# Reordered small work in a software-pipelined attention and Fourier kernel: maskings, a last fold, square roots, input requests and the work behind the last product

## The chip, the cores and the metric

The kernel runs on one core of one Trainium2 chip. The metric is the device time of an execution in microseconds (us). Of several executions the median counts; beside it there is one execution that was profiled, and all durations of single instructions come from that one.

## The reference

Threshold attention, whose output goes through a Fourier mixing, a layer norm and a two-layer channel network. The sizes are B = 8 batches, H = 8 heads, S = 576 tokens, D = 64, so the width is 512, and the hidden width of the network is 2048. All data are float32.

```python
scores = q @ k.transpose(0, 1, 3, 2) / sqrt(64)             # [8, 8, 576, 576]
scores = where(scores >= max(scores, -1) - tau, scores, -1e9)
attn = exp(scores - max(scores, -1))
attn = attn / (sum(attn, -1) + 1e-9)
x = (attn @ v).transpose(0, 2, 1, 3).reshape(8, 576, 512)

u = x + real(fft(fft(x, axis=1), axis=2))
un = (u - mean(u, -1)) / sqrt(var(u, -1) + 1e-6)
out = u + maximum(un @ w1, 0) @ w2                          # w1 512x2048, w2 2048x512
```

## The kernel before, in words

**One loop over attention steps, with the rest fitted in between.** Two heads form a pair; there are 32 pairs (four a batch). The 576 queries of a pair are cut into five steps: t = 0 to 3 take 128 queries of each head, t = 4 the last 64 of both. So a batch has 20 steps, numbered i = 0 to 159 over all, with n = i // 5 the pair and t = i % 5. Batch 0 (`step`) and batch 1 (`second_batch`) also load and prepare the weights. From batch 2 on (about 400 us into the profile, when `late` is set) the loop at L1587 runs, once per step, with these parts in this order:

1. `scores` (L427): q times k into PSUM buffers `sc`, of which there are two.
2. `softmax_first`: VectorE takes the row maxima (L506), ScalarE the exponentials (L512), from the same `sc`.
3. `values_in_parts`: after t = 2 and t = 4 the weights of a half pair times v (`pv`, L627), copied by ScalarE to `x` or, for the batch's first pair, `x_first` (L634).
4. `fill()`, explained below.
5. `softmax_second`: VectorE masks the exponentials (L527; it reads `sc` as well and so sets it free) and makes the reciprocals of the sums.
6. `weights_in_parts`: TensorE transposes the weights of the step before (`pe` and `pw`, L578 and L596), ScalarE copies them out (L584, L598). A second `fill()` lies between its parts.
7. `softmax_third`: ScalarE divides (L540). At t = 1 `prep_ends` copies the last queries, at t = 2 `scale_q` scales the next pair's q, at t = 3 `prep_pair` transposes the next pair's k and q on VectorE (L398 to L401) and then calls `load_pair(n + 1)`.
8. A third `fill()`.

`load_pair` (L134) issues eight transfers for q and k of a pair, `load_v` (L149, L152) four for v. All of them stand in the queue of the SyncE engine, in program order, along with the weight loads and the stores of the output. `q_in` and `k_in` have one buffer each, which the transposes read; `v_in` has two.

**Folding and mixing.** After each pair `fold_rows` makes the symmetric sums and differences of x that the Fourier products need, into `f`. It is a generator, moved on by `fold_more()` at fixed places. It runs on GpSimd (POOL in the profile), but for the last pair of each batch on VectorE; that last one is spread over the first steps of the next batch, and at step i % 20 == 2 `start_batch` makes the batch's mixing available. `mixing(b)` first combines the four chunks of `f` on VectorE (`fold_chunks` L709 and L710, then L735, L731, L740), then multiplies by the table over the width (`py`, L750), over the tokens (`pa`, L767), forms `low` and `high` in a shared buffer `tmp` (L787, L788), and adds x, on GpSimd, into `u_t`, the transposed u (the inner function `add`, L790 and L794), chunk by chunk: chunks 0 and 3 in the first of two rounds, 1 and 2 in the second.

**Channel network in the background.** The tokens are cut into nine groups of 512, g = 0 to 8. Group 0 is computed plainly (`channels`), the others by `two_level`, which replaces each product by seven on sums of quarters, twice over. A *first stretch* makes 28 blocks of the hidden layer (`ph`, L1161). Its right operands, differences of quarters of `u_t`, are made by `u_form` on GpSimd (L1085; one goes to `t_room`), and VectorE empties the banks by additions (L1098). A *second stretch* has seven products of seven blocks each (`po`, L1278), emptied by ScalarE copies or VectorE additions (L1292, L1295) into five vectors `v_u`, `v_11`, `v_22`, `v_21`, `v_12` of 7 x 128 columns. `gather` (L1209) sums the seven columns of a vector to results, `finish` adds these to u (L861), `rows.store` sends the rows out (L868). The left operands are made ahead by `l2_forms` (L1142, VectorE and GpSimd) and `l1_form` (L1119). Small jobs are hung at slots of a product (`at_slots(at, (jn, ...), jobs)`, run after block jn of product number at), or put into the list `pending`, of which `tick()` does two after each block of the next first stretch. `rows.load` (L834 to L843) transposes u back and takes its mean and variance; `rows.factors` takes the square root (L850), calls one exponential so that the table of ScalarE is back (L853), and the reciprocal on VectorE (L854).

The weight forms of `two_level` lie in DRAM (`f1`, `f2`) and come in loads of four blocks, 1 MB each (`w<-f`, L1034), into three buffers in turn. `block` asks for a load two ahead.

**What sets the order.** The instruction order is written out by hand: each engine works through its own instructions in program order, and waits for others by semaphores. `fill()` adds a share to a budget and does one part of the mixing, then blocks of the background (`work`) until the budget is spent:

```python
    def fill():
        nonlocal budget, spent
        budget += per_slot
        if mixes:
            mix(1)
        while work and spent < budget and work[0][0] < mixed:
            done = next(work[0][1], None)
```

A group of batch b can start when that batch's mixing is done (`mixed`). Behind the last step, the last mixing and the rest of the groups are done by the loop at L1635, with no attention work left between.

PSUM has four banks for everything but the scores (`mm`), taken in turn.

Of the kernel before, what the change touches and what calls it, by code (L numbers as in the profile page):

```python
# [47 lines left out]
def kernel(  # L48
# [12 lines left out]
    nc = tc.nc  # L61
# [4 lines left out]
    NPAIR = H // 2  # L66
# [324 lines left out]
    def prep_pair(n):  # L391

        q_raw, k_raw = loaded.pop(n)
        kT = sb.tile([128, D + S], FP32, tag="kT", name="kT")
        nc.vector.transpose(kT[:, D : D + S], k_raw[:, :])  # L398
        nc.vector.transpose(kT[64:128, 0:D], k_raw[64:128, 512:S])
        qT = sb.tile([128, S], FP32, tag="qT", bufs=1, name="qT")  # L400
        nc.vector.transpose(qT[:, :], q_raw[:, :])  # L401
        heads[n] = (qT, kT, v_in[n % 2])
        if n + 1 < B * NPAIR:
            load_pair(n + 1)
# [314 lines left out]
    def mixing(b):  # L719
# [58 lines left out]
        for t in range(2):  # L778
# [9 lines left out]
            nc.vector.tensor_tensor(out=high, in0=pa[:, 0:KH], in1=sin, op=ALU.add)  # L788
            def add(c, rows, first, second, eng=nc.gpsimd):
                eng.tensor_tensor(  # L790
# [269 lines left out]
    def two_level(g, rows):  # L1060
# [22 lines left out]
        def u_form(out_, in0, in1):  # L1083
            for c in range(2):
                nc.gpsimd.tensor_tensor(  # L1085
                    out=out_[:, c], in0=in0[:, c], in1=in1[:, c], op=ALU.subtract
                )
# [111 lines left out]
        for _ in forms:  # L1199
            pass  # L1200
        while pending:
            tick()
        if g == 1:
            for part in range(4):
                s1_part(part)
# [20 lines left out]

        def finish(i, n, v):
            v = v.rearrange("p (j n) -> p j n", n=128)
            cols = slice(256 * n, 256 * n + 256)
# [35 lines left out]
        at_slots(2, (0, 1, 2, 3, 4), gather(P, v_11))  # L1265
        at_slots(4, (0, 2), finish(0, 0, v_11))
        at_slots(
            5, (0,), [lambda: P.tensor_tensor(out=v_12, in0=v_u, in1=v_22, op=ALU.add)]
        )
        at_slots(6, (0, 1), [plus(P, v_22, v_u), plus(P, v_21, v_u)])  # L1270
        for at, m in enumerate(L1):
            for jn, j in enumerate(J):
                if jn in (0, 4):
                    bank = ps.tile([128, 512], FP32, tag="mm", bufs=4, name="po")
                to = bank[:, 128 * (jn % 4) : 128 * (jn % 4 + 1)]
                right_ = block(g, True, 7 * at + jn)
                for s in range(4):
                    nc.tensor.matmul(  # L1278
                        to, lefts[m][j][:, s], right_[:, 128 * s : 128 * (s + 1)],
                        start=jn in (0, 4) and s == 0, stop=s == 3, skip_group_check=True,  # L1280
                    )
                if jn in (3, 6):
                    size = 512 if jn == 3 else NV - 512
                    src = bank[:, 0:size]

                    def here(v):
                        return v[:, 0:512] if jn == 3 else v[:, 512:NV]

# [4 lines left out]
                    else:  # L1293
                        to = here(v_12 if m == 3 else v_u)
                        V.tensor_tensor(out=to, in0=to, in1=src, op=ALU.add)  # L1295
                for job in side.get((at, jn), ()):
                    job()
                if jn == 3 and at < 4:
                    rows.load((2, 3, 0, 1)[at])
                    if at == 3:  # L1300
                        rows.factors()
                    yield ND * 128
# [3 lines left out]
            if m != 3:  # L1306
                yield 2048
        last = g == NG - 1
        for v in (v_22, v_21, v_12):
            pending.extend(gather(V if last else P, v))  # L1310
        pending.extend(finish(1, 1, v_22))
# [3 lines left out]
        pending.append(stores(0, 1))  # L1315
        if g == NG - 1:
            while pending:
                tick()
        yield 2048

    pending = []

    def tick():

        for _ in range(2):
            if pending:
                pending.pop(0)()

# [14 lines left out]

    late = []


# [5 lines left out]

    def fill():
        nonlocal budget, spent
        budget += per_slot
        if mixes:
            mix(1)
        while work and spent < budget and work[0][0] < mixed:
            done = next(work[0][1], None)
            if done is None:  # L1360
                work.pop(0)
            else:
                spent += done

    total = B * per_batch
# [221 lines left out]
    for i in range(2 * per_batch, total + 3):  # L1587
# [16 lines left out]
        if i % per_batch == 2:  # L1604
            while folds:
                fold_more()
            start_batch(i // per_batch - 1)
        if t == 1 and n + 1 < B * NPAIR:
            load_v(n + 1)
        fill()  # L1610
        if t == 1:
            folds.append(fold_rows(n - 1))
        if i < total:
            softmax_second(i)
        weights = weights_in_parts(i - 1) if i <= total else iter(())
        next(weights, None)
        if t > 2 or i % per_batch == 1:
            fold_more()
        fill()
        if i % per_batch == 1:  # L1620
            fold_more()
        next(weights, None)
        if i < total:
# [5 lines left out]
            if t == 3 and n + 1 < B * NPAIR:  # L1629
                prep_pair(n + 1)  # L1630
        if i % per_batch == 1:
            fold_more()
        fill()
    per_slot = cost(0) / 40
    while mixes or work:  # L1635
# [47 lines left out]
```

## Time and profile before

| | |
|---|---|
| median of 9 runs | 1615.22 us (1612.22 to 1617.65) |
| profiled execution | 1617.93 us, of which its span is 1616.2 us |
| TensorE clock granted, mean over the span | 0.984 |
| instructions | 27099 |
| busy: TensorE matmul, TensorE weight load | 1543.8 us (96%), 1191.5 us (74%) |
| busy: VectorE, ScalarE, GpSimd | 1085.0 (67%), 907.1 (56%), 827.3 us (51%) |
| transfers | 239.05 MB, on average 148 GB/s |

In the profile PE stands for TensorE, PEld for its weight loads, DVE for VectorE, ACT for ScalarE, POOL for GpSimd, SP for SyncE; SPq is the issue of a transfer in SyncE's queue. A line as `PE sc L427 <- DVE e L527: 6.4, 6, 2.7` in the list of waits says: TensorE, about to do the product at line 427 into `sc`, waited for VectorE's operation at line 527 that writes `e`, 6.4 us in all, 6 times, the longest 2.7 us. In the timeline a line has start, duration, engine, source line, operation and the number of instructions put together in it; in brackets stands the idle time ahead of it and what ended that.

### The profile page before, as it was taken

The numbers are of one execution on the slowest core, as the hardware profiler recorded it, in microseconds if no ns is written. First come the engines' busy times: TensorE is split into PE (matmuls) and PEld (weight loads), VectorE is DVE, ScalarE is ACT, GpSimd is POOL, SyncE is SP. The second block draws the span as 40 slices with busy tenths as digits, with TensorE's granted clock in tenths as the row PEclk, the third lists the DMA queues.
The fourth block names the chain that finished last, engine by engine and source line by source line (L and its number), as shares of the span: only waits on it lengthen the run. The fifth ranks groups of instructions, "written<-read, shape, count | busy, mean of one in ns | idle before, by whom it ended". The sixth has DMA issues, their size and how long they took to land.

```text
span 1616.2 us, 27099 instructions
## 1 busy us (share of the span) xinstructions
PE 1543.8 (96%) x9770; PEld 1191.5 (74%) x9770; DVE 1085.0 (67%) x2141; ACT 907.1 (56%) x1873; POOL 827.3 (51%) x1035
## 2 busy tenths in 40 slices
PE   8999889999999999999999999999999999899997
PEld 4555445555787777877787878787887778879997
DVE  7997786855867666776567566856676656536446
ACT  5775665544664566656766576666665665123121
POOL 6784664034454542646254724554264526547746
PEclk9999999999999999999999999999999999999999
DMA  6423221555945344644455345545453435446655
GB/s 159 128 57 114 74 75 36 178 153 155 280 133 209 107 143 137 190 122 133 140 156 156 118 128 153 175 122 161 127 180 108 145 112 179 167 152 234 235 196 187
DMA packets 245499, 239.05 MB, mean 148 GB/s; under 512 B 196947, under 2 KB 214869, under 8 KB 225014
## 3 DMA queue, kind: packets, MB, share of 16 engines
q1 hardware_dynamic: 242854, 237.02, 47.7%
q8 instruction: 78, 1.28, 0.3%
q10 hardware_dynamic: 2512, 0.30, 0.2%
q14 instruction: 55, 0.45, 0.1%
HBM read 207.50 MB, written 29.62 MB: 147 GB/s over the span
## 4 chain that ended last, share of the span: by engine, by line
PE 74%; DVE 14%; ACT 4%; DMA 3%; issue 2%; POOL 2%; SPq 1%; DVEq 0%; ACTq 0%; POOLq 0%
PE ph L1161 23%; PE po L1278 18%; PE pv L627 8%; PE sc L427 7%; PE pw L596 6%; PE po L899 3%; PE ph L875 2%; DVE e L467 2%; PE sc L433 1%; PE py L750 1%; DVE neg L506 1%; ACT e L512 1%; PE pa L767 1%; DVE e L527 1%; DVE neg L451 1%
## 5 line engine op out<-in xcount | busy, mean ns | idle before, releaser
L512 ACT ACTIVATE e<-sc,neg 128x576 f32<-128x576 f32 x216 | 158.6, 734 | 137.4 <-DVE neg L506 137.4
L1278 PE MATMUL po<-w,w_all 128*128 128x128 f32 x1792 | 230.0, 278 | 4.0 <-DMA w<-f 4.0
L506 DVE TENSOR_REDUCE neg<-sc 128x1 f32<-128x576 f32 x216 | 154.0, 750 | 111.9 <-PE sc L427 106.1
L1278 PEld LDWEIGHTS po<-w,w_all 128*128 128x128 f32 x1792 | 214.9, 194 | 12.9 <-issue 11.0
L1098 DVE TENSOR_TENSOR hs<-ph,hs 128x512 f32<-128x512 f32 (+1 forms) x128 | 105.2, 822 | 172.8 <-PE ph L1161 118.0
L1107 POOL TENSOR_TENSOR w<-hs 128x512 f32<-128x512 f32 x32 | 41.7, 1307 | 323.0 <-ACT hs L1103 249.7
L427 PE MATMUL sc<-kT,qT 64*128 64x288 f32 x1024 | 175.7, 436 | 16.1 <-DVE e L467 8.5
L596 PE MATMUL pw<-ident,e 128*128 128x128 f32 x1152 | 170.8, 275 | 14.0 <-ACT x_first L634 5.7
L1161 PE MATMUL ph<-u_t,w 128*128 128x256 f32 x768 | 180.5, 381 | 0.7 <-DMA w<-f 0.5
L598 ACT COPY e_t<-pw 128x512 f32<-128x512 f32 x256 | 147.7, 592 | 51.9 <-PE pw L596 50.5
L527 DVE SCALAR_TENSOR_TENSOR e<-sc,thr,e 128x576 f32<-128x576 f32 x216 | 168.1, 811 | 12.4 <-ACT thr L516 12.4
L540 ACT ACTIVATE e<-e,den 128x576 f32<-128x576 f32 x216 | 157.7, 776 | 30.3 <-DVE den L534 29.6
L596 PEld LDWEIGHTS pw<-ident,e 128*128 128x128 f32 x1152 | 135.6, 141 | 33.2 <-ACT x_first L634 7.5
L1161 PEld LDWEIGHTS ph<-u_t,w 128*128 128x128 f32 x768 | 141.2, 190 | 23.5 <-issue 4.9
L1161 PE MATMUL ph<-w_all,w 128*128 128x256 f32 x672 | 156.4, 382 | 0.0
L427 PEld LDWEIGHTS sc<-kT,qT 64*128 64x128 f32 x1024 | 95.8, 188 | 74.4 <-issue 31.9
L1161 PEld LDWEIGHTS ph<-w_all,w 128*128 128x128 f32 x672 | 123.8, 190 | 21.7 <-issue 6.4
L1103 ACT ACTIVATE hs<-hs 128x512 f32<-128x512 f32 (+1 forms) x96 | 74.1, 771 | 113.9 <-DVE hs L1098 112.9
L1209 POOL TENSOR_TENSOR w_all<-w_all 128x128 f32<-128x128 f32 (+2 forms) x161 | 117.5, 747 | 23.7 <-DVE w_all L1295 10.2
L1278 PE MATMUL po<-w,hs 128*128 128x128 f32 x960 | 126.9, 279 | 0.0
L1278 PEld LDWEIGHTS po<-w,hs 128*128 128x128 f32 x960 | 116.9, 194 | 5.1 <-issue 3.3
L790 POOL TENSOR_TENSOR u_t<-x,tmp 128x289 f32<-128x289 f32 (+1 forms) x47 | 34.5, 734 | 98.9 <-DVE tmp L787 98.9
(217 smaller groups left out, 2984.4 us busy)
## 6 DMA issues: line engine op xcount, KB each, us to landing
w<-f SPq DMA_DIRECT2D x152, 1024.0 KB, 4.9
hs<-in_moe_w_ch_dram SPq DMA_DIRECT2D x23, 512.0 KB, 4.6
q_in<-in_q_dram SPq DMA_DIRECT2D x128, 72.0 KB, 2.4
out_dram<-u SPq DMA_DIRECT2D x36, 256.0 KB, 2.3
k_in<-in_k_dram SPq DMA_DIRECT2D x124, 72.0 KB, 2.5
v_in<-in_v_dram SPq DMA_DIRECT2D x64, 128.0 KB, 2.5
f<-w SPq DMA_DIRECT2D x14, 512.0 KB, 3.3
f<-w SPq DMA_DIRECT2D x7, 1024.0 KB, 4.3
```

What stands on the lines that cost most here:

```text
L427: nc.tensor.matmul(sc[j][:, c, 0:HALF], qT[hp, 128 * t : 128 * t + 128], kT[hp, k0 + HALF * c : k0 + HALF * (c + 1)], start=True, stop=True,)
L506: nc.vector.tensor_reduce(out=neg[:, j : j + 1], in_=sc[j][:, :, 0:HALF], axis=AXIS_XY, op=ALU.max, negate=True,)
L512: nc.scalar.activation(out=ej, in_=sc[j][:, :, 0:HALF], func=ACT.Exp, bias=neg[:, j : j + 1], scale=1.0)
L527: nc.vector.scalar_tensor_tensor(out=ej, in0=sc[j][:, :, 0:HALF], scalar=thr[:, j : j + 1], in1=ej, op0=ALU.is_ge, op1=ALU.mult, accum_out ...
L540: nc.scalar.activation(out=e[:, S * j : S * (j + 1)], in_=e[:, S * j : S * (j + 1)], func=ACT.Copy, scale=den[:, j : j + 1],)
L596: nc.tensor.transpose(pw[:, c, :], e[:, c0 : c0 + 128], ident[:, :])
L598: nc.scalar.copy(e_t[:, 4 * j : 4 * j + 4, qs], pw[:, :, :])
L627: nc.tensor.matmul(pv[64 * j : 64 * j + 64, 0:m], vt[:, 2 * c + j, :], e_t[:, 4 * j + c, 0:m] if c < 4 else ends[:, 0, 0:m], start=(c == 0 ...
L1098: nc.vector.tensor_tensor(out=to, in0=bank, in1=to if other is None else other, op=ALU.add)
L1161: nc.tensor.matmul(bank[:, 256 * q : 256 * q + 256].rearrange("p (two n) -> p two n", two=2), left[:, 256 * c + 128 * q : 256 * c + 128 * ...
L1209: return lambda: eng.tensor_tensor(out=to, in0=to, in1=other, op=ALU.add)
L1278: nc.tensor.matmul(to, lefts[m][j][:, s], right_[:, 128 * s : 128 * (s + 1)], start=jn in (0, 4) and s == 0, stop=s == 3, skip_group_check ...
```

## The change

Taken in the order of the diff:

- **Requests.** In the late loop `load_pair` is no longer called by `prep_pair` but at the end of t = 4, and `load_v` not ahead of the first `fill()` of t = 1 but at the end of t = 2.
- **Last mixing.** The additions into `u_t` of batch 7 are made on VectorE for chunks 1 and 3. Behind the last step (`ended`), `fill()` does background blocks first and a part of the mixing after them.
- **Right operands.** For the last two groups `u_form` is on VectorE.
- **Held jobs.** In the first `fill` of a step the jobs at slots and those of `tick()` are collected in the list `held` and done behind `softmax_second`; the mixing's part of that `fill` comes behind them. So the maskings stand directly behind the exponentials.
- **Last fold.** The fold of a batch's last pair has a generator of its own, `last_fold`, stepped at fixed places: once behind the masking of step i % 20 == 1, twice more in that step, and the rest behind the maxima of step i % 20 == 2.
- **Square root.** `rows.factors` is called behind `softmax_third`, or by the first `finish` that needs it, by way of the list `wanted`.
- **Behind the last product.** In the last group, the gathers and additions of `v_22`, `v_21` and `v_12` lie at slots of the last product instead of behind it, and the addition `v_22 += v_u` moves from GpSimd to VectorE. The last product's blocks 4, 5 and 6 get a bank each and are emptied one by one. `finish(0, 0, v_11)` moves two slots later, in all groups.

```diff
@@ prep_pair
-        if n + 1 < B * NPAIR:
+        if n + 1 < B * NPAIR and not late:
             load_pair(n + 1)
@@ mixing
-            def add(c, rows, first, second, eng=nc.gpsimd):
+            def add(c, rows, first, second, eng=None):
+                if eng is None:
+                    eng = nc.vector if b == B - 1 and c % 2 else nc.gpsimd
@@ two_level, u_form
-                nc.gpsimd.tensor_tensor(
+                (nc.vector if g >= NG - 2 else nc.gpsimd).tensor_tensor(
@@ two_level, finish
+            if wanted:
+                wanted.pop().factors()
@@ two_level, slots
-        at_slots(4, (0, 2), finish(0, 0, v_11))
+        at_slots(4, (2, 4), [lambda n=n: finish(0, 0, v_11)[n]() for n in range(2)])
-        at_slots(6, (0, 1), [plus(P, v_22, v_u), plus(P, v_21, v_u)])
+        if g < NG - 1:
+            at_slots(6, (0, 1), [plus(P, v_22, v_u), plus(P, v_21, v_u)])
+        else:
+            at_slots(6, (0, 0), [plus(V, v_22, v_u), plus(P, v_21, v_u)])
+            at_slots(6, (1, 1, 1, 1, 1), gather(V, v_22))
+            at_slots(6, (2, 2), finish(1, 1, v_22))
+            at_slots(6, (2, 2, 3, 3, 3), gather(V, v_21))
+            at_slots(6, (4, 4), finish(1, 0, v_21))
+            at_slots(6, (4,), [stores(2, 3)])
+            w = v_12.rearrange("p (j n) -> p j n", n=128)
+            at_slots(6, (4,) * 4, [
+                plus(V, w[:, 1:5:3], twice(w[:, 0])), plus(V, w[:, 6], w[:, 2]),
+                plus(V, w[:, 6], w[:, 4]), lambda: rows.add(0, slice(256, 384), w[:, 1]),
+            ])
...
+            at_slots(6, (5,) * 4, [
+                plus(V, w[:, 5], w[:, 4]), plus(V, w[:, 2:4], twice(w[:, 5])),
+                lambda: rows.add(1, slice(256, 512), second), stores(1),
+            ])
@@ two_level, the products
+                cut = g == NG - 1 and m == 3
-                if jn in (0, 4):
+                if jn in (0, 4) or cut and jn > 4:
                     bank = ps.tile([128, 512], FP32, tag="mm", bufs=4, name="po")
...
-                for job in side.get((at, jn), ()):
-                    job()
+                while held:
+                    held.pop(0)()
+                held.extend(side.get((at, jn), ()))
+                while held and not holding:
+                    held.pop(0)()
                 if jn == 3 and at < 4:
                     rows.load((2, 3, 0, 1)[at])
                     if at == 3:
-                        rows.factors()
+                        wanted.append(rows)
...
-        last = g == NG - 1
+        if g == NG - 1:
+            w = v_12.rearrange("p (j n) -> p j n", n=128)
+            rows.add(0, slice(384, 512), w[:, 6])
+            rows.store(0)
+            return
         for v in (v_22, v_21, v_12):
-            pending.extend(gather(V if last else P, v))
+            pending.extend(gather(P, v))
@@ tick
+        while held:
+            held.pop(0)()
         for _ in range(2):
             if pending:
-                pending.pop(0)()
+                held.append(pending.pop(0))
+        while held and not holding:
+            held.pop(0)()
@@ fill
-    def fill():
+    def fill(hold=False):
         nonlocal budget, spent
+        holding[:] = [True] if hold else []
         budget += per_slot
-        if mixes:
+        if mixes and not ended and not hold:
             mix(1)
         while work and spent < budget and work[0][0] < mixed:
...
+        holding.clear()
+        if mixes and ended:
+            mix(1)
@@ the late loop
         if i % per_batch == 2:
-            while folds:
-                fold_more()
+            for _ in last_fold:
+                pass
             start_batch(i // per_batch - 1)
-        if t == 1 and n + 1 < B * NPAIR:
-            load_v(n + 1)
-        fill()
-        if t == 1:
-            folds.append(fold_rows(n - 1))
+        fill(True)
         if i < total:
             softmax_second(i)
+        while held:
+            held.pop(0)()
+        if mixes:
+            mix(1)
+        if t == 1:
+            if n % NPAIR:
+                folds.append(fold_rows(n - 1))
+            else:
+                last_fold = fold_rows(n - 1)
+                next(last_fold)
         weights = weights_in_parts(i - 1) if i <= total else iter(())
         next(weights, None)
-        if t > 2 or i % per_batch == 1:
+        if t > 2:
             fold_more()
         fill()
         if i % per_batch == 1:
-            fold_more()
+            next(last_fold)
...
+        if wanted:
+            wanted.pop().factors()
         if i % per_batch == 1:
-            fold_more()
+            next(last_fold)
         fill()
+        if t == 2 and n + 1 < B * NPAIR:
+            load_v(n + 1)
+        if t == 4 and n + 2 < B * NPAIR:
+            load_pair(n + 2)
+    ended.append(True)
```

## The prediction

> **What bounds the kernel now.** I read engine busy time first, then the waits of TensorE from 400 us on (the change acts in the loop over batches 2 to 7 and in what follows it), then the timeline at each long wait.
>
> ```profile
> PE 1543.8 (96%) x9770; PEld 1191.5 (74%) x9770; DVE 1085.0 (67%) x2141; ACT 907.1 (56%) x1873; POOL 827.3 (51%) x1035
> ```
>
> ```profile
> PE sc L427 <- DVE e L527: 6.4, 6, 2.7
> PE pw L596 <- ACT x_first L634: 5.7, 4, 1.4
> PE py L750 <- DVE f L731: 5.0, 2, 4.6
> PE ph L1161 <- POOL t_room L1085: 4.1, 1, 4.1
> PE po L1278 <- DMA w<-f: 4.0, 1, 4.0
> ```
>
> TensorE is the bound: 96% busy, and from 400 us on only five causes stop it for 4 us or more in total. No product is added or removed, so the change can only win these 25 us, the tail behind the last product, and what a stop costs in clock. That cost shows here:
>
> ```profile
> 482.78 0.83 PE L1278 MATMUL po<-w,w_all 128*128 128x128 f32 x6
> 487.62 1.62 PE L1278 MATMUL po<-w,w_all 128*128 128x128 f32 x6 [4.01 <-DMA w<-f]
> ```
>
> Six passes take 0.83 us before the stop and 1.62 us after it: half speed. By the windows query, the mean granted clock is 0.62 in 484 to 493 us, 0.53 in 1390 to 1397.2 and 0.50 in 1417.6 to 1421, behind the three stops over 4 us. The DMA stop comes from SyncE's queue:
>
> ```profile
> 465.39 0.32 SPq L1034 DMA_DIRECT2D w<-f  x1
> 477.87 1.95 SPq L134 DMA_DIRECT2D q_in<-in_q_dram  x4
> 479.87 2.55 SPq L134 DMA_DIRECT2D k_in<-in_k_dram  x4
> 482.52 1.44 SPq L1034 DMA_DIRECT2D w<-f  x3
> ```
>
> Between 465.4 and 477.9 the queue stands before the q request (it waits for the transposes L401); three weight loads behind it leave together, too late. The two other long stops:
>
> ```profile
> 1391.37 0.80 PE L750 MATMUL py<-dim_c,f 128*128 128x128 f32 x2 [4.56 <-DVE f L731]
> ```
>
> ```profile
> 1418.09 2.50 PE L1161 MATMUL ph<-t_room,w 128*128 128x256 f32 x5 [4.09 <-POOL t_room L1085]
> ```
>
> And the tail, VectorE alone behind the last product:
>
> ```profile
> 1602.96 2.09 POOL L1209 TENSOR_TENSOR w_all<-w_all 128x896 f32<-128x896 f32 x1
> ...
> 1604.86 0.55 DVE L1295 TENSOR_TENSOR w_all<-w_all,po 128x384 f32<-128x384 f32 x1 [1.99 <-PE po L1278]
> 1605.33 4.66 DVE L1209 TENSOR_TENSOR w_all<-w_all 128x256 f32<-128x256 f32 x15
> 1609.90 2.46 DVE L861 SCALAR_TENSOR_TENSOR u<-w_all,rstd,u 128x256 f32<-128x256 f32 x6
> 1611.24 1.80 SPq L868 DMA_DIRECT2D out_dram<-u  x4
> ```
>
> [...] stops of 1.4 us (at 1050.5) brought none while 2.7 us (at 695) did, so I take about 2 us as my own threshold. [...] the 512-wide L1142 on VectorE takes 0.69 us alone and 2.55 us at 1595.3, beside a GpSimd addition of 2.08 us. [...]
>
> **The change part by part.**
>
> *Later requests.* Eight q and k requests (4.5 us of SyncE's queue by the view above) move from the transposes at t = 3 to the end of t = 4, four v requests (2.2 us, 0.5 to 0.6 each) from t = 1 to the end of t = 2. By then what they overwrite is read, so the queue does not stand (before: 135.5 us at L134 and 63.5 us at L149 from 400 us on), and the built order puts three weight loads ahead of this q request. Queued behind them stay the next weight loads; they are asked for two loads ahead, so 4.5 us fits. The new data is needed two to three steps later, at 8.6 us a step (20 steps from 1041.9 to 1214.5), and lands in 2.5. Gain: 4.0 of stop and half of the 5.0 us from 487.6 to 492.6: **6.5**.
>
> *u_t additions and right operands.* For batch 7, chunk 3's additions (four instructions, 2.8 us at 0.7) go from GpSimd to VectorE, for the last two groups all eight right-operand subtractions too. GpSimd ran its first twelve additions from 1407.96 to 1417.3, and t_room only then. Now eight are left, and chunk 3 at t = 0 runs beside chunk 0, so the shared tmp is free 1.4 us earlier. t_room needs chunks 0 and 1: done about 1411.9, two subtractions of at most 0.7 on VectorE bring 1413.3; TensorE arrives at 1413.5. The next operand needs chunk 2's last row (1414.7 plus 0.7), TensorE wants it at 1415.3. Behind these eight on VectorE stand bank-emptying additions L1098; four banks cover about 3 us. Gain: 4.1 plus 1.5 for eight passes in 3.4 instead of 1.9: **5.6**; bounds 3 and 6.
>
> *Last mixing behind the steps.* The folds f (L731) keep their place in VectorE's chain from 1372.4 to 1391.3; the square root only moves inside it. But products are issued first now: three more blocks (24 passes at 0.11 = 2.65 us) stand ahead of the waiting py. The stop falls from 5.0 to about 2.4, and of 2.9 us half-clock loss about 1.3 goes. Gain **3.9**; bounds 1 and 7.
>
> *Maskings, last fold, square root.* Steps 1 to 3 of each batch (1031 to 1051 is typical) hold the stops sc (0.6, once 2.7), ends (0.6) and pw (1.4). Masks move ahead of folding and of held side jobs, so sc's and ends' stops go. But pw waits for the bank of x_first, whose copy stands on ScalarE behind the exponentials of step 3, and these behind L506 on VectorE. Up to that L506, VectorE works from 1033.5 to 1047.8 without a break, and before and after have the same instructions in that stretch. The reciprocal's wait for the square root (0.70 ahead of the masks) comes back later: between the division and the reciprocal ScalarE now has two L540 (1.5) and a table load (1.28) and 0.30, VectorE only 2.3 us of fold, so about 0.9. So L506 of step 3 stays, and the stop collects at pw. What is won is one more block of products ahead of py: 0.95 a batch for five batches, less one or two half clocks of 1.7, as pw's stop grows to about 2.2. Gain **2**; bounds: none of the stops comes back, 15; half clock in all six batches that have these steps, minus 6. The early f-to-w store order (around 410 us) is taken at zero, bounded by a 1.2 us stop there.
>
> *Short work behind the last product.* Fifteen gathers and six u additions (4.66 + 2.46) spread over the last product. But VectorE gets the 896-wide v_22 addition (0.69 x 896/512 = 1.2), cannot start before v_u at 1600.6, and is locked out by GpSimd's 2.09 for v_21. From 1600.6: 0.4 + 1.2 + 2.1 = 1604.2; then two gathers 3.0, three pairs' additions 2.4 less a third (2.1 with narrow pieces), emptying 0.6 and three times 0.25, v_12's gathers 1.75: ends about 1612.5, against 1612.36. What follows the end, a store and 3.8 us, is the same. Gain **0**; bounds 3 (lock never hit) and minus 1.
>
> Sum: 6.5 + 5.6 + 3.9 + 2 + 0 = 18. The profiled execution took 1617.9 (span 1616.2 and 1.7 around it), so 1599.9; the nine runs' median, 1615.2, stands 2.7 below it: **1597**.
>
> **The rivals.** A change within 0.2% (3.2 us) could not be told from none.
> - *Forecast* (0.56): as summed, 1597.
> - *VectorE's chain shortens* (0.22): [...] the two-input folds meet the lock less often (L710 takes 1.74 at 1039, 0.79 at 1381.6), and stops at sc, ends and pw all go: 11 us more, and 3 in the tail: 1583. For it: the lock costs 1 to 2 us a batch there. Against it: the fold still meets L1119.
> - *Gains half given back* (0.10): half clock at each collected pw stop (minus 6 instead of 2), last mixing at 1, tail minus 1: 6.5 + 5.6 + 1 - 6 - 1 = 6: 1609.
> - *Slower* (0.08): [...] two windows at half clock follow (3.4 lost) and the stop itself adds 1.5; six batches give 29, against 16 from the first three parts: 1628. It decides from 3.2 us a batch. Against it: L506's place does not move.
> - *Not what it says* (0.04): in step 1 row statistics and in others emptying additions still stand ahead of the masks, and the weight loads are late for another reason: 1614.
>
> Faster 0.88 (the first three), same 0.04, slower 0.08. Range 1581 to 1610: its lower end takes in the second case, its upper the third; what is left out has 0.12.
>
> **What the changed profile would show.** Right: no TensorE wait for w<-f over 1 us and no L134 wait on qT; ph's wait on t_room under 0.5; py on f about 2.4; sc on e gone, and pw on x_first grown to 2 or more in each batch; VectorE's last u addition 7 to 8 us behind the last product. Wrong: if pw's wait stays at 1.4 or vanishes, L506 did come earlier and I am too slow; if half clock appears six times more, too fast; if w<-f still stops TensorE, the queue was not the cause.

## The result, and the profile after

| | before | after |
|---|---|---|
| median | 1615.0 us (31 runs) | 1606.12 us (10 runs, 1604.21 to 1607.74) |
| ratio to before, 95% interval | | 0.9944 [0.9936, 0.9952] |
| span of the profiled execution | 1616.2 us | 1605.7 us |
| granted TensorE clock, mean | 0.984 | 0.985 |

The changed kernel is 9 us faster (0.56%). The forecast was 1597 within 1581 to 1610: the direction and the range held, but half of the forecast gain of 18 us is missing. The busy times of the changed kernel:

```profile
PE 1540.9 (96%) x9770; PEld 1190.7 (74%) x9770; DVE 1105.8 (69%) x2165; ACT 908.0 (57%) x1873; POOL 812.2 (51%) x1014
```

VectorE has 21 us more and GpSimd 15 us less. The waits of TensorE from 400 us on, the same view as before:

```profile
PE pw L596 <- ACT x_first L634: 9.0, 5, 2.2
PE pe L578 <- DVE w_all L1326: 5.2, 5, 2.6
PE py L750 <- DVE f L731: 2.9, 1, 2.9
PE ph L1163 <- DVE hs L1100: 2.1, 2, 1.8
PE pw L596 <- ACT ends L584: 1.5, 3, 0.5
PE ph L1163 <- DVE w_all L1087: 1.0, 1, 1.0
```

(From L790 on, lines of the changed kernel stand two or more lower: L790 is now L792, L1161 is L1163, L1098 is L1100, L1278 is L1306, L1295 is L1326.) The waits on `e`, on `t_room` and on the weights have left the list. But `pw` on `x_first` grew from 5.7 to 9.0 us, and `pe` and `ph` now wait for VectorE's emptying additions (L1326, L1100). Added up, the whole view falls from 30.5 to 25.2 us. The clock gave nothing: between 400 us and the last product both executions spend 20.5 us at half clock. Where the change wins and where it loses has to be looked for place by place.

**A ledger of the two profiled executions.** Every step begins with `sc` products, in the same order in both kernels, so the difference of their start times says where time was won or lost:

| stretch (time of before) | forecast | measured |
|---|---|---|
| up to step 40 (0 to 288 us), where the two kernels' code is alike | 0 | -1.95 |
| steps 40 to 59 (to 477 us) | 0 | -1.1 |
| steps 59 to 61: the weight loads | -6.5 | -6.6 |
| steps 61 to 159: batches 3 to 7 | -2 | **+3.9** |
| last pv to first ph of group 7: last mixing | -3.9 | -2.3 |
| that first stretch, 224 products | -5.6 | **-2.1** |
| then to the last product; behind it | 0 | 0; -0.3 |
| sum | -18 | -10.5 |

The first row is no effect of the change: in the executions shown below, all with the same code up to there, it lies between -2.9 and +0.7. The two bold rows are what is missing.

SyncE's queue around the place of the lost 4.0 us:

```profile
462.36 18.52 SPq L1036 DMA_DIRECT2D w<-f  x4
480.99 2.99 SPq L134 DMA_DIRECT2D q_in<-in_q_dram  x4
```

Four weight loads go out ahead of the q request, the three that had stood behind it among them, and TensorE does not stop. Step 3 of batch 6, TensorE's timeline:

```profile
1039.33 0.83 PE L750 MATMUL py<-dim_c,f 128*128 128x65 f32 x6
1040.72 0.30 PE L578 MATMUL pe<-ident,e 128*128 128x128 f32 x1 [0.56 <-DVE w_all L1326]
1043.20 0.84 PE L596 MATMUL pw<-ident,e 128*128 128x128 f32 x4 [2.19 <-ACT x_first L634]
1043.84 1.12 PE L750 MATMUL py<-dim_s,f 128*128 128x128 f32 x4
```

Between 1040.2 and 1043.2 us TensorE does one transpose. The view of busy time and clock by windows shows what follows:

```profile
1043.50:1046.90 3.40, 3.40 (x19) 2.62 (x17) 3.29 (x10) 2.56 (x7) 0.00 (x0) 0.51 0.03 7
```

(The columns after the window are its length, then busy time and instructions of PE, PEld, DVE, ACT and POOL, then the clock, the busy share of the DMA engines and GB/s.) TensorE is busy for the whole window and does 19 products, at clock 0.51. The same happens from 521.3, 695.4 and 1217.6 us, so in batches 3, 4, 6 and 7. In the kernel before there is one such window in these batches, from 697.4 us in batch 4.

The first stretch of group 7, TensorE and then VectorE:

```profile
1405.71 1.89 PE L1163 MATMUL ph<-t_room,w 128*128 128x256 f32 x8
1408.57 2.77 PE L1163 MATMUL ph<-w_all,w 128*128 128x256 f32 x10 [0.96 <-DVE w_all L1087]
```

```profile
1404.79 0.74 DVE L1087 TENSOR_TENSOR t_room<-u_t 128x256 f32<-128x256 f32 x2
1407.52 1.76 DVE L1087 TENSOR_TENSOR w_all<-u_t,t_room 128x256 f32<-128x256 f32 x2 [1.98 <-POOL u_t L792]
1409.21 1.27 DVE L1087 TENSOR_TENSOR w_all<-u_t,w_all 128x256 f32<-128x256 f32 x2
1410.40 1.54 DVE L1087 TENSOR_TENSOR w_all<-u_t 128x256 f32<-128x256 f32 x2
```

`t_room` is in time now. The second operand (`w_all<-u_t,t_room`) is not: VectorE waits 1.98 us for GpSimd's chunk 2, and TensorE stops. The rest of the subtractions runs to 1411.9, and only then VectorE empties banks.

The tail, VectorE's last work:

```profile
1590.42 4.71 DVE L1213 TENSOR_TENSOR w_all<-w_all 128x896 f32<-128x896 f32 x6
...
1601.90 0.35 DVE L863 SCALAR_TENSOR_TENSOR u<-w_all,rstd,u 128x128 f32<-128x128 f32 x1
```

The last product ends at 1594.6, VectorE at 1602.25: 7.6 us behind it, where it was 7.5. The gathers now run beside the last product, the first of these lines being the 896-wide addition and the first gathers, but VectorE, at work almost without a break from 1589.25 on, is not done sooner.

### The profile page after: what moved, and what is told of

Read it like the earlier page. It is cut to its first block, busy times and chain, and to the rows that moved or that the text cites. A ratio compares the mean times of both kernels' runs of the same rounds, so it can differ in the third digit from the quotient of the medians.

```text
span 1605.7 us, 27061 instructions
## 1 busy us (share of the span) xinstructions
PE 1540.9 (96%) x9770; PEld 1190.7 (74%) x9770; DVE 1105.8 (69%) x2165; ACT 908.0 (57%) x1873; POOL 812.2 (51%) x1014
## 3 DMA queue, kind: packets, MB, share of 16 engines
q8 instruction: 78, 1.28, 0.3%
## 4 chain that ended last, share of the span: by engine, by line
PE 75%; DVE 15%; ACT 4%; issue 2%; DMA 2%; POOL 1%; SPq 1%; DVEq 0%; ACTq 0%; POOLq 0%
PE ph L1163 24%; PE po L1306 17%; PE pv L627 8%; PE sc L427 7%; PE pw L596 6%; PE po L901 4%; PE ph L877 2%; DVE e L467 2%; PE py L750 2%; PE sc L433 1%; PE pa L767 1%; DVE neg L451 1%; PE pe L578 1%; PE pa L771 1%; ACT e L512 1%
## 5 line engine op out<-in xcount | busy, mean ns | idle before, releaser
L506 DVE TENSOR_REDUCE neg<-sc 128x1 f32<-128x576 f32 x216 | 154.0, 750 | 113.2 <-PE sc L427 105.7
L1306 PE MATMUL po<-w,w_all 128*128 128x128 f32 x1792 | 228.7, 278 | 0.7 <-ACT ends L584 0.7
L1306 PEld LDWEIGHTS po<-w,w_all 128*128 128x128 f32 x1792 | 214.3, 193 | 10.2 <-issue 5.5
L1100 DVE TENSOR_TENSOR hs<-ph,hs 128x512 f32<-128x512 f32 (+1 forms) x128 | 105.2, 822 | 157.6 <-PE ph L1163 104.3
L1163 PE MATMUL ph<-u_t,w 128*128 128x256 f32 x768 | 180.5, 381 | 0.7 <-DMA w<-f 0.6
L427 PE MATMUL sc<-kT,qT 64*128 64x288 f32 x1024 | 171.3, 433 | 9.5 <-DVE e L467 9.0
L596 PEld LDWEIGHTS pw<-ident,e 128*128 128x128 f32 x1152 | 137.5, 143 | 36.3 <-ACT x_first L634 10.1
L1163 PE MATMUL ph<-w_all,w 128*128 128x256 f32 x672 | 157.0, 382 | 2.9 <-DVE hs L1100 1.8
L1163 PEld LDWEIGHTS ph<-u_t,w 128*128 128x128 f32 x768 | 141.2, 190 | 23.5 <-issue 4.5
L1163 PEld LDWEIGHTS ph<-w_all,w 128*128 128x128 f32 x672 | 123.5, 190 | 25.6 <-issue 6.2
L1306 PE MATMUL po<-w,hs 128*128 128x128 f32 x960 | 126.3, 279 | 0.0
L1306 PEld LDWEIGHTS po<-w,hs 128*128 128x128 f32 x960 | 116.2, 193 | 9.4 <-issue 7.2
L792 POOL TENSOR_TENSOR u_t<-x,tmp 128x289 f32<-128x289 f32 (+1 forms) x45 | 34.0, 755 | 106.4 <-DVE tmp L787 106.4
```

The lines of the kernel that those rows point to most:

```text
L427: nc.tensor.matmul(sc[j][:, c, 0:HALF], qT[hp, 128 * t : 128 * t + 128], kT[hp, k0 + HALF * c : k0 + HALF * (c + 1)], start=True, stop=True,)
L506: nc.vector.tensor_reduce(out=neg[:, j : j + 1], in_=sc[j][:, :, 0:HALF], axis=AXIS_XY, op=ALU.max, negate=True,)
L596: nc.tensor.transpose(pw[:, c, :], e[:, c0 : c0 + 128], ident[:, :])
L1100: nc.vector.tensor_tensor(out=to, in0=bank, in1=to if other is None else other, op=ALU.add)
L1163: nc.tensor.matmul(bank[:, 256 * q : 256 * q + 256].rearrange("p (two n) -> p two n", two=2), left[:, 256 * c + 128 * q : 256 * c + 128 * ...
L1306: nc.tensor.matmul(to, lefts[m][j][:, s], right_[:, 128 * s : 128 * (s + 1)], start=(jn in (0, 4) or cut and jn > 4) and s == 0, stop=s == ...
```

## The experiments

Each was timed beside the kernel before. The theory after the result: the parts gain what they gain alone, and the moved maskings (with the last fold and the square root) lose, since they only gather small stops of TensorE into one of about 2.2 us, behind which the clock was 0.51 (step 3 of batch 6). The rivals: the parts disturb each other, or the weight loads and folds have other causes.

**One part of the change alone, and all but the maskings.**

```diff
# e1_requests: before, with
@@ prep_pair
-        if n + 1 < B * NPAIR:
+        if n + 1 < B * NPAIR and not late:
@@ late loop
-        if t == 1 and n + 1 < B * NPAIR:
-            load_v(n + 1)
...
+        if t == 2 and n + 1 < B * NPAIR:
+            load_v(n + 1)
+        if t == 4 and n + 2 < B * NPAIR:
+            load_pair(n + 2)
# e2_vector: before, with
+                    eng = nc.vector if b == B - 1 and c % 2 else nc.gpsimd
+                (nc.vector if g >= NG - 2 else nc.gpsimd).tensor_tensor(
# e3_order: before, with
+        if mixes and not ended:
             mix(1)
         while work and spent < budget and work[0][0] < mixed:
...
+        if mixes and ended:
+            mix(1)
# e4_no_masks: after, with fill(), fold_more(), rows.factors() and the slots
# (0, 2) of finish(0, 0, v_11) as before had them
```

> The kernel before with one part of the change: q, k at the end of t = 4, v at the end of t = 2. Theory (SyncE's queue stood before the q request and held three weight loads): the wait of TensorE for w<-f of 4.0 us at 483 us and its half clock go, nothing else moves: 6.6 us less than before, as the starts of the steps show between step 59 and step 61 of the changed kernel (ratio 0.996). Rival (the loads were late because of the memory traffic, and another part of the change removed that): the wait stays, ratio within 0.9993 and 1.

> The kernel before with one part of the change: chunks 1 and 3 of batch 7's additions into u_t, and the right operands of the last two groups, on VectorE. Theory (the operands no longer wait for GpSimd's twelve additions, but the bank-emptying additions now queue behind them on VectorE): the wait for t_room of 4.1 us goes, one of about 1 us on the operands and one of 1.8 us on hs come, no half clock: 2.1 us less than before (ratio 0.9987), the amount by which the 224 products of that first stretch got shorter in the changed kernel. Rival (the loss of 3.5 us against the forecast of 5.6 comes from the new order of the last mixing): 5.6 us less, ratio 0.9965.

> The kernel before with one part of the change: behind the last step the background's blocks come before each part of the mixing. Theory: the wait of py for f falls from 4.6 to about 3 us by the blocks that now stand ahead of it, and both half-clock windows stay: 2.3 us less (ratio 0.9986). Rival (the shorter wait came from the moved square root in VectorE's chain): the wait stays at 4.6, no change.

> The changed kernel without the held jobs, the own last fold and the moved square root (these three as before). Theory (with the maskings moved ahead, VectorE's chain through steps 1 to 3 of a batch is no shorter, so the stops collect at x_first's bank[...] and cost half clock): the waits are those of before (sc on e, pw on x_first 1.4 each), no half clock at 521, 1043 and 1217 us; by the starts of the steps the moved parts cost 3.9 us in batches 3 to 7 and win 1.1 in batch 2, so this kernel is 2.8 us faster than the changed one: ratio to before 0.9926. Rival (the later transfers disturb those steps, and the maskings help): slower than the changed kernel by 1 to 3 us, ratio 0.995 to 0.9965.

| kernel | ratio [95%] | us against before (ratio less 1, times 1615.2) | trace: rows of the ledger it touches |
|---|---|---|---|
| e1_requests | 0.9953 [0.9941, 0.9965] | -7.6 | weight loads -6.6; steps 44 to 55 -2.4 |
| e2_vector | 0.9987 [0.9980, 0.9993] | -2.1 | 224 products 54.2 to 52.1 us: -2.1 |
| e3_order | 0.9973 [0.9963, 0.9983] | -4.4 | last mixing 41.3 to 36.3 us: -4.9 |
| e4_no_masks | 0.9916 [0.9902, 0.9929] | -13.6 | steps 61 to 159: +1.5 |
| the change | 0.9944 [0.9936, 0.9952] | -9.0 | steps 61 to 159: +3.9 |

The three parts add up to 14.1 us, and the kernel that has all three and the new tail gains 13.6: within the noise they don't disturb each other. The rival for the weight loads falls, since e1 alone ends that stop. e4 is faster than the full change, and the intervals don't overlap: **the maskings, fold and square root cost about 4.5 us together** (with them the two moved slots of `finish(0, 0, v_11)`, which e4 also puts back). The forecast had them at a gain of 2. In the ledger 2.4 of it lie in steps 61 to 159 and 1.5 in steps 44 to 55. Steps 61 to 159 are +1.5 in e4 as they are +1.4 in e1, which has the code of before there: both executions have two half-clock windows in batch 4, that of before one. The same step of e4, TensorE's timeline:

```profile
1037.80 0.27 PE L578 MATMUL pe<-ident,e 128*128 128x128 f32 x1
1039.49 0.66 PE L596 MATMUL pw<-ident,e 128*128 128x128 f32 x4 [1.42 <-ACT x_first L634]
```

The stop is 1.42 us, as in the kernel before, and full clock follows (1.00 from 1039.5 to 1042.9, 28 products).

The expectation for e3 was too small, and e4 shows why. Both have the same order behind the last step and the same stop there (2.6 us), but their clocks differ, first e3 and then e4, each over the 6.8 us from within the stop on:

```profile
1385.80:1392.60 6.80, 5.33 (x45) 4.84 (x45) 4.75 (x6) 1.27 (x3) 4.88 (x4) 1.00 0.33 137
```

```profile
1379.80:1386.60 6.80, 6.19 (x29) 6.20 (x30) 4.14 (x6) 1.25 (x3) 4.88 (x4) 0.50 0.25 106
```

45 products at full clock against 29 at half, behind stops of the same length. The whole last mixing takes 36.3 us in e3 and 38.8 in e4.

**Which of the moved parts loses, and whether the place of the copy to x_first does it.**

```diff
# e5_x_early: after, and e6_x_early_no_masks: e4, each with
         next(values, None)
+        if i % per_batch == 3:
+            next(values, None)
         if i < total:
             softmax_first(i)
# e7_held_only: e4, with fill(True), the held jobs and mix(1) behind softmax_second
# e8_root_only: e4, with wanted.append(rows) and wanted.pop().factors() behind softmax_third,
#   and the slots (2, 4) of finish(0, 0, v_11)
```

> The changed kernel with one more edit: at step i % 20 == 3 the copy of pv to x_first stands ahead of the exponentials in ScalarE's order instead of behind them (ScalarE is idle there for 4 us). Theory (the maskings' gain collects at x_first's bank, because its copy queues behind exponentials that wait for VectorE): pw no longer waits there; the next bank, that of the first py, still waits for its copy behind the exponentials, so about 1.1 us a batch comes back, and the half clock of 1.7 us in batches 3, 4, 6 and 7: 8 to 12 us less than the changed kernel, ratio to before 0.987 to 0.989. Rival (VectorE's chain itself delays the steps, whatever bank is waited for): the stop moves whole to the next bank, 0 to 2 us less, ratio 0.993 to 0.9945.

> As the kernel without the held jobs, own last fold and moved square root, with the earlier copy to x_first at step i % 20 == 3. Theory: the four stops of 1.4 us at pw go, and little takes their place, since the first py was copied by 1040 us in that order: 5 us less than without the edit (ratio to before 0.9885). Rival: the stops move to the next bank, no more than 1 us less (0.991).

> The kernel without the held jobs, own last fold and moved square root, with the held jobs alone put back (maskings directly behind the exponentials, a part of the mixing behind them). Theory (the loss comes from taking away the stops at sc and ends, which collect at pw): pw's wait for x_first grows from 1.4 to over 2 with half clock, 3 to 4.5 us slower than without them, ratio to before 0.994. Rival (the moved square root or fold, not the maskings, lengthens VectorE's chain): within 1 us of the kernel without them, 0.9912 to 0.9922.

> The kernel without the held jobs, own last fold and moved square root, with the moved square root alone put back. Theory (VectorE's reciprocal no longer waits 0.7 us ahead of the maskings, but the time is only taken from one stop and given to the next): at most 1 us either way, ratio to before 0.991 to 0.9922. Rival (the square root's two table loads, now between the divisions and the next exponentials, are what costs): 3 to 4.5 us slower, ratio 0.9935 to 0.9945.

| kernel | ratio [95%] | stop at step 3 of batch 6 | half-clock windows, 500 to 1300 us | steps 61 to 159 |
|---|---|---|---|---|
| e4 | 0.9916 [0.9902, 0.9929] | 1.42 | 2 | +1.5 |
| e7, held jobs | 0.9928 [0.9913, 0.9943] | 2.06 | 6 | +3.3 |
| e8, square root | 0.9931 [0.9916, 0.9947] | 1.82 | 4 | +4.7 |
| the change | 0.9944 [0.9936, 0.9952] | 0.56 and 2.19 | 4 | +3.9 |
| e5, change with early copy | 0.9919 [0.9905, 0.9933] | 0.57 and 2.00 | 4 | +2.7 |
| e6, e4 with early copy | 0.9911 [0.9895, 0.9926] | 1.23 | 2 | +0.3 |

The held jobs alone and the square root alone each lengthen the stop at `pw` and bring two to four half-clock windows more. By the medians they cost 1.9 and 2.4 us. Their intervals overlap e4's, so singly they are shown by the traces only. The last fold was not tried alone.

Whether the longer stop costs, or the half clock behind it, shows when the row of steps 61 to 159 is cut by batch (us against before; in brackets the half-clock windows behind the stops of its steps 1 to 3, of which before has one, in batch 4):

| kernel | batch 3 | batch 4 | batch 5 | batch 6 | batch 7 |
|---|---|---|---|---|---|
| the change | +1.6 (1) | +0.9 (1) | -0.6 (0) | +0.9 (1) | +1.0 (1) |
| e4 | 0.0 (0) | +1.5 (2) | 0.0 (0) | 0.0 (0) | 0.0 (0) |
| e7, held jobs | +0.7 (1) | +0.9 (2) | +0.4 (1) | +0.7 (1) | +0.7 (1) |
| e8, square root | +0.4 (0) | +1.2 (2) | +1.6 (1) | +1.6 (1) | 0.0 (0) |

In batch 5 the changed kernel has the same stop as in batch 6, but full clock behind it:

```profile
871.12 0.66 PE L596 MATMUL pw<-ident,e 128*128 128x128 f32 x4 [2.19 <-ACT x_first L634]
```

```profile
872.90:876.30 3.40, 3.40 (x28) 3.00 (x28) 3.25 (x7) 2.40 (x6) 1.27 (x1) 1.00 0.00 0
```

There the moved parts win 0.6 us, and in batch 6 they lose 0.9: the half clock is worth 1.5 us a batch and turns the gain into a loss. In e8 the stop is 1.8 us in batches 5, 6 and 7 alike; it costs nothing in batch 7, where full clock follows, and 1.6 in the others. So e8's theory, at most 1 us, held for the stop and left out the clock. Its rival, the two table loads (1.28 us each in the profiles of before and after), falls: they are there in batch 7 too, and in batch 6 the exponentials behind them still wait 0.25 us for the maxima.

The mean clock recorded for every execution says the same beyond the profiled ones. What an execution lost to half clock, (1 - clock) times its span, is 21.0 us on average in the 15 executions of the changed kernel (e10 below is five of them) and 17.0 in the five of e4. That is about 4 of the 4.5 us. For e8 (17.4 in six) the same sum doesn't show it, so e8's part rests on its trace.

The early copy was a miss. In e5 the wait on `x_first` is gone, and the next one has come in its place:

```profile
1040.91 0.60 PE L596 MATMUL pw<-ident,e 128*128 128x128 f32 x4
1043.52 0.71 PE L750 MATMUL py<-dim_s,f 128*128 128x128 f32 x4 [2.00 <-ACT y_e L760]
```

The first `pw` runs 2.3 us sooner, and the next `py` stops for the bank whose copy (`y_e`) also stands behind the exponentials. Of the 8 to 12 us expected, e5 shows 4 by the ratios (1.2 in the ledger's row; the profiled execution was the slowest of its six), and e6 of its 5 us less than 1 (e4's and e6's intervals overlap). The sizes are nearer the rival's, and its mechanism is what the traces show: what delays these steps is VectorE, which works without a break up to its maxima L506 (in the changed kernel the exponentials stand 4.22 us for them), and each bank on ScalarE is only the place where that shows.

**The right operands, and the change once more.**

```diff
# e9_third_on_pool: e4, and e11_both: e6, each with
-        u_form(t3, b[1, 1], b[0, 1])
+        u_form(t3, b[1, 1], b[0, 1], nc.gpsimd)
-                (nc.vector if g >= NG - 2 else nc.gpsimd).tensor_tensor(
+                (eng or (nc.vector if g == NG - 2 else nc.gpsimd)).tensor_tensor(
# e10_changed_again: the changed kernel
```

> The kernel without the held jobs, own last fold and moved square root, in which fewer right-operand subtractions are on VectorE: in group 7 the first three pairs stay there, the fourth (two subtractions) goes back to GpSimd, which has nothing urgent after 1402.8 us; group 8's all go back. Theory (what was missing of the forecast 5.6 us is that the bank-emptying additions, and ScalarE's relu and copy behind them, queue behind eight subtractions): VectorE reaches its first emptying addition 1.46 us earlier, the wait of ph for hs falls from 1.8 to about 0.4, the 224 products take 50.7 us instead of 52.1, the whole 1.4 us less: ratio to before 0.9907. Rival (the additions wait for something else): the stretch stays at 52.1 us.

> The changed kernel once more, to have it on the same chip as the others, and to see a second execution's clock. Theory [...]: the waits are the same to 0.1 us, the places and number of the half-clock windows differ; ratio to before 0.9944, within 0.9936 to 0.9952. Rival (half clock is tied to the stop): the same windows behind the same stops.

> Without the held jobs, own last fold and moved square root; with the earlier copy to x_first; and with the fourth right operand of group 7 and all of group 8 on GpSimd. Theory: 1.4 us less than without the last of these, and by the trace of that kernel little from the copy (its stop of 1.4 us moves to the first py's copy): ratio to before 0.9895 to 0.9905. Rival (VectorE is not what delays them): 0.9911 or more.

| kernel | ratio [95%] | 224 products of group 7 |
|---|---|---|
| e9_third_on_pool | 0.9919 [0.9906, 0.9933] | 53.4 us |
| e11_both | 0.9919 [0.9907, 0.9932] | 53.4 us |
| e10_changed_again | 0.9950 [0.9937, 0.9963] | 52.1 us |

e9 and e11 miss: not 50.7 but 53.4 us. The wait for `hs` did fall, to 0.3 us, so the subtractions on VectorE were what delayed the emptying. But e9's TensorE, VectorE and GpSimd show another cost:

```profile
1405.58 4.78 PE L1163 MATMUL ph<-w_all,w 128*128 128x256 f32 x13 [3.01 <-DVE w_all L1087]
```

```profile
1402.49 3.54 DVE L1087 TENSOR_TENSOR w_all<-u_t,t_room 128x256 f32<-128x256 f32 x2 [1.99 <-POOL u_t L792]
```

```profile
1403.07 1.40 POOL L1087 TENSOR_TENSOR w_all<-u_t 128x256 f32<-128x256 f32 x2
```

The two subtractions took 1.76 us in the changed kernel and 3.54 here. Beside them GpSimd's last addition, its two new subtractions and a gather follow one another without a gap from 1402.4 on. A single subtraction took 0.67 us at 1405.95; so by my estimate the first of the two ended near 1405.4 (1402.49 and 3.54, less one of 0.67), only behind the fourth of those operations (near 1405.1, the gathers taking 0.64 each). It is the same kind of delay as the prediction had measured on L1142 (0.69 us alone, 2.55 beside an addition of GpSimd), its "lock"; the expectation of e9 did not use it. Behind the stop of 3.0 us TensorE did 13 products in 4.78 us, 0.37 each, where the 8 ahead of it took 1.89, 0.24 each: a half-clock window at 1406.

e10 repeats the change's ratio within its interval, with the same waits to 0.1 us. The half-clock windows, however, stand behind the same stops in both executions, so its rival is not refuted by this run. The grid on which the recorded clock changes (measured in the last section) lies 1.25 us otherwise against the first instruction, but against the start of step 59 the two executions agree to 0.05 us, so this pair tests little. The rival is refuted by e3 against e4 and by batch 5 above.

**A version that covers the last mixing.** What is left behind the last step is the stop of 2.6 us at `py` and the half clock that it can bring.

```diff
# e12_more_ahead: e6, with
     ended.append(True)
+    budget += 6 * 2048
```

> The kernel with the earlier copy to x_first and without held jobs, own last fold and moved square root, with one more edit: behind the last step the budget starts six blocks higher, so all 24 background products that lay between the parts of the last mixing stand ahead of the first py. Theory (the stop of 2.7 us at py <- f lasts as long as VectorE's folds, and 24 products at 0.11 us cover it[...]): the stop falls to under 0.3 us, the stretch from the last pv to the first ph of group 7 falls from 37.5 us to 33 to 34, with no half clock in it: 3.5 to 4.5 us less, ratio to before 0.9885. Rival (the py products then wait for their banks, whose copies on ScalarE had been hidden by those 24 products): new waits of py on y_e or y_o take 2 us or more of it back, ratio 0.990 to 0.991.

It measured 0.9896 [0.9880, 0.9913], a median of 1597.54 us: 16.8 us less than before, and faster than the changed kernel. The place in its TensorE timeline, and the clock:

```profile
1380.80 1.16 PE L1306 MATMUL po<-w,w_all 128*128 128x128 f32 x8 [0.30 <-POOL w_all L1144]
1382.11 0.94 PE L750 MATMUL py<-dim_c,f 128*128 128x65 f32 x6 [0.16 <-DVE w_all L1326]
1382.88 0.61 PE L750 MATMUL py<-dim_s,f 128*128 128x128 f32 x4
```

```profile
1376.00:1392.00 16.00, 15.30 (x120) 13.61 (x119) 10.61 (x14) 4.01 (x11) 10.56 (x7) 1.00 0.56 198
```

No wait over 0.3 us is left there, the clock is whole, the `py` products follow each other without new waits, and the stretch takes 34.0 us instead of 37.5 in e6, as expected. The expectation counted 24 products moved ahead; by the traces they are 40. By the ratios the gain over e6 is 2.4 us, short of the 3.5 expected, and the two intervals overlap, so this last edit alone is shown by its trace only.

## Why the prediction was right or wrong

**Later requests: right.** 6.5 was forecast, 6.6 measured. One sign failed: SyncE still waits for the transposes L401, 35.6 us in 5 places instead of 135.5 in 19, but no weight load that is due stands behind them. What the prediction took at zero, bounded by 1.2, was worth 2.4 us in e1 (steps 44 to 55). Four v transfers stood there ahead of the stores of weight forms, and VectorE waited 2.3 us for such a store ahead of the masks (at 412.8 us). In e1 both the wait and the stop of `sc` behind it are gone. In the full change 1.0 of the gain is left. In e6, e9 and e11, which have this edit too, it is 1.5, so its size varies.

**Right operands: the step that failed is "Gain: 4.1 plus 1.5 ... 5.6".** It was 2.1, below the lower bound of 3. Two terms were mis-sized. The second operand was to be ready 5.1 us after the first `ph` and came after 6.4: GpSimd and VectorE both work on `u_t` there, and GpSimd's L792 took 1.58 us at 1404.5 against 0.80 at 1402.9. And "four banks cover about 3 us" of the emptying additions did not hold: behind eight subtractions they cost a stop of 1.8 us. No half clock came.

**Last mixing: right mechanism, within its bounds of 1 and 7.** The stop fell to 2.9 us (2.4 forecast). The gain was 2.3 in the profiled execution, with half clock after the stop, and 4.9 in e3 without; 3.9 lies between.

**Maskings, last fold, square root: the wrong sign.** The mechanism was named ("the stop collects at pw", L506 stays), and it is what happened. L506 of step 3 in batch 6 came 7.3 us earlier than before, while the batch's start came 7.65 us earlier: it did not gain. The step that failed is the size, "0.95 a batch for five batches, less one or two half clocks of 1.7". The block of products brought 0.6 where no half clock followed (batch 5), and half clock followed in four batches of five, at about 1.5 us each, where before had it in one. From +2 that is to about -4.5 by e4; the bound given was -6. The third case of the rivals, half clock at each collected stop, was the right story for this part, and with 1609 nearer than the forecast.

VectorE's chain did not stay the same either. From the maskings of step 1 to L506 of step 3 it grew from 17.8 to 19.1 us, and `pe` got a stop of its own in front of `pw`. The fold in batch 6, before and after:

```profile
1033.51 1.78 DVE L678 TENSOR_TENSOR half<-x 128x287 f32<-128x287 f32 x2
```

```profile
1024.66 2.81 DVE L678 TENSOR_TENSOR half<-x 128x287 f32<-128x287 f32 x2
```

The fold now starts just as GpSimd starts two operations L1121 (2.7 us), and a later one (L690) takes 1.12 us instead of 0.15 beside a third. L710 takes 0.79 instead of 1.74, as the second rival said. So that rival was right for one operation, and others met GpSimd in its place. The 0.9 us wait for the square root did not come back: VectorE has no idle time there, since the fold took it.

**Tail: right.** 0 was forecast and 0.3 measured; VectorE's end lay 7 to 8 us behind the last product as said.

**The sum.** The point was 9 us too low: 3.5 us from the operands, 6 from the maskings' sign, and smaller ones against each other. That the third rival's 1609 came so near is in part luck: it had the operands at 5.6 and the tail at -1, where 2.1 and 0.3 were measured.

## What to carry to other kernels

A stop of the bounding engine is not removed by moving it: ask which wait ends last after the change, and add the clock to its price. Stops of 0.6 to 1.4 us cost only themselves here, while the same time gathered into one of about 2.2 us cost 1.5 us more in four batches of five. What helped was independent work put ahead of the waiting product (e12: 40 products stand where 2.6 us of waiting was) and a queue cleared for what is due (e1). Before work goes to the other elementwise engine, look at what queues behind it there, and at what the two engines then do at the same time (e9: two subtractions took 3.54 us beside GpSimd's work instead of 1.76).

## What the runs showed of the hardware

The prediction took "about 2 us" as the length of a stop that brings half clock. It is not the stop's length alone: behind the same stop of 2.19 us the clock was 0.51 in batch 6 and 1.00 in batch 5.

In the profiles of before and after, up to the last product, half clock lasted 3.4 us (the changed kernel: 0.50 from 521.3 to 524.7) or twice that (0.50 from 1384.9 to 1391.7). The recorded clock changes of an execution lie on a grid of 3.41 us (to 0.06 us), whose place against the first instruction differs between these 14 executions (from 0.0 to 3.3 us). I laid that grid over TensorE's timelines (400 to 1560 us; gaps under 0.25 us left out) and added up the idle time in each window, a window being one stretch of the grid, that was itself at full clock. Windows with 1.84 us or more were followed by half clock in 39 of 39 cases, those with 1.55 to 1.83 us in 8 of 20, those with 1.0 to 1.54 us in 1 of 52. The limits were drawn from these same windows, and many of them are one stop seen in several executions. The changed kernel alone has five of the first kind (2.93, 2.62, 2.75, 2.21 and 1.87 us, half clock behind each) and two of the second (1.66 and 1.83 us, full clock behind both).

So in these executions about half a window of idle time was enough every time. In all 39 one stop alone filled it; whether pieces add up is not shown (one window with 0.74 and 0.85 us was followed by half clock). A stop of 2.6 us cost nothing more where the grid cut it in two (e3: 1.4 and 1.2 us; e9: 1.6 and 1.0), and one or two windows at half speed where most of it lay in one (e6 one, e4 two). The one case of the 52 is an exception to this: in the kernel before, the stop of 2.7 us at 695 us was cut into 1.3 and 1.4 us, and half clock followed. What sets the place of the grid is not shown.
